# Block attention followed by a token-mixing MLP: another tiling, and an emission order made by a list scheduler

## The chip, the cores and the metric

The kernel runs on one core of one Trainium2 chip. The metric is device time in microseconds. Kernel before: 179.93 us, the median of three runs (179.21 to 181.21).

## The reference, cut to what matters

```python
# q, k, v: (8, 8, 576, 64) fp32; batch 8, heads 8, tokens 576, head size 64
q_c, k_c, v_c = (x.reshape(B, H, 9, 64, 64) for x in (q, k, v))    # chunks of 64 tokens
scores = matmul(q_c, k_c.transpose(0, 1, 2, 4, 3)) / sqrt(64)
attn = exp(scores - max(scores, axis=-1))
attn = attn / (sum(attn, axis=-1) + 1e-09)
x = matmul(attn, v_c).reshape(B, H, S, D).transpose(0, 2, 1, 3).reshape(B, S, 512)

wq, wk = x @ w_q, x @ w_k                                          # w_q, w_k: (512, 64)
W_tok = einsum('bsd,btd->bst', wq, wk) / sqrt(64)
mixed = einsum('bst,btd->bsd', W_tok, x)
out = maximum(mixed, 0.0) @ w_out                                  # w_out: (512, 512), out fp32
```

Both kernels compute the mixing as wq times G, where G = wk^T x is 64 by 512 for each batch, so that no 576 by 576 matrix is made.

## The kernel before

All matmul operands are fp16; inputs are cast by the loads, which POOL issues through its one queue (`load`, lines 77 to 108). A batch's q and k come as runs of two tokens (512 bytes of fp32), its v as runs of one token (256 bytes). Six buffers of q, k and v hold batches 0 to 5; batches 6 and 7 are loaded into buffers that come free. The first two batches are cut into pieces of tiles, each piece with its own transfers for q, k and v and for each half of the heads; weights go between them. The identity for the transposes is made ahead of the first load.

The attention is cut into 36 units. The token rows of four heads (a half, `sl`) are strung together into one row, and a unit is eight 64-token chunks of that row in each of the two halves, 16 blocks of 64 by 64 in all. A unit passes through these stages; two units' first stages are emitted ahead, and the loop over `kk` emits the stages of three neighbouring units in a fixed pattern:

- `stage_a1`, `stage_a2`: 16 transposes of 128 by 64 on TensorE (L327, tile `tp`), one copy of 1,024 columns on VectorE (L337, `qkt`).
- `stage_b1`, `stage_b2`: 16 score matmuls of 64 by 64 (L351, `sp`); maximum (L359, `mx`) and subtraction (L365, `sh`) on VectorE; exponential on ScalarE (L373, `es`).
- `stage_c`: four transposes of 128 by 128 (L380, `ep`) and their copy on ScalarE (L382, `et`).
- `stage_d1`, `stage_d2`: 16 matmuls with v, which has a column of ones that yields the sum (L395, `xp`); sum, reciprocal and product on VectorE (L407, L409, L410, into `x_nat`).

For each batch, the token-mixing part (`make_moe`) follows: transposes of x and copies on ScalarE (L143, L150, `xt`), the projections to wq and wk transposed (L163 and L166, `wpa`, `wpb`; copies L173, L174 into `wqkT`), a copy of wq to the other 64 partitions (L176, `wqd`), ten transposes that turn wk back (L190 to L193, `wknp`; copy L195, `wkn`), G (L205, L209, `gp`; copy L213, `g16`), mixing (L225, `ma`, and L245, `mb`, for the last 64 tokens; relu L131 on ScalarE), and the output projection (L261, `op`; copy L269; tails L281, L289), stored through SyncE's queue from four buffers `osb`. The steps of this part have a period and a place in the loop written out by hand (`plan`, `fill`), with costs in microseconds that decide how many output tiles fit into a period; what is left at the end is emitted by due time.

PSUM: one bank each for `tp`, `sp` and `ep`, two for `xp`, three in rotation for all tiles of the token-mixing part. Every engine runs its instructions in the order of emission.

Of the kernel before, what the change touches and what calls it, by code (L numbers as in the profile page):

```python
# [12 lines left out]
ALU = mybir.AluOpType  # L13
AX = mybir.AxisListType


@with_exitstack
def kernel(
# [10 lines left out]

# [4 lines left out]
    CH = 64  # L38
    P = 128
    HQ = H // 2  # L40
    NC_ = S // CH
    NI = HQ * NC_
    NT = NI // 4
    NS = NI // 2
    NU = B * NI // 8
    R, G = 2, 32
    scale_attn = 1.0 / math.sqrt(D)
    scale_moe = 1.0 / math.sqrt(DH)
    ds = bass.ds

    const = ctx.enter_context(tc.tile_pool(name="const", bufs=1))
    qn_pool = ctx.enter_context(tc.tile_pool(name="qn", bufs=6))
    v_pool = ctx.enter_context(tc.tile_pool(name="vpool", bufs=6))
    qkt_pool = ctx.enter_context(tc.tile_pool(name="qkt", bufs=3))
    sm_pool = ctx.enter_context(tc.tile_pool(name="smp", bufs=3))
    e_pool = ctx.enter_context(tc.tile_pool(name="epool", bufs=3))
    xt_pool = ctx.enter_context(tc.tile_pool(name="xtp", bufs=2))
    moe_pool = ctx.enter_context(tc.tile_pool(name="moep", bufs=2))
    osb_pool = ctx.enter_context(tc.tile_pool(name="osb", bufs=4))

    PS = bass.MemoryType.PSUM
    t_psum = ctx.enter_context(tc.tile_pool(name="tps", bufs=1, space=PS))
    s_psum = ctx.enter_context(tc.tile_pool(name="sps", bufs=1, space=PS))
    et_psum = ctx.enter_context(tc.tile_pool(name="etps", bufs=1, space=PS))
    x_psum = ctx.enter_context(tc.tile_pool(name="xps", bufs=1, space=PS))
    m_psum = ctx.enter_context(tc.tile_pool(name="mps", bufs=3, space=PS))


    ctx.enter_context(tc.manual_schedule())

    ident = const.tile([P, P], F16, name="ident")
    make_identity(nc, ident[:])

    x_nat = const.tile([P, B * NS, 2, D], F16, name="x_nat")
    x_bat = x_nat[:].rearrange("p (b w s) l d -> p b w s l d", b=B, w=2)

    def load(b, cuts):
        qn = [
            qn_pool.tile([P, 2, NT, R * D], F16, name=f"qn{ti}", tag=f"qn{ti}")
            for ti in range(2)  # L80
        ]
        vt = v_pool.tile([P, 2, NS, D + 2], F16, name="vt", tag="vt")
        flat = [
            x[b].rearrange("h s d -> (h s) d").rearrange("(l t p r) d -> l p t (r d)", l=2, p=P, r=R)
            for x in (q, k)
        ]
        vflat = v[b].rearrange("h s d -> (h s) d").rearrange("(l n p) d -> l p n d", l=2, p=P)
        nc.gpsimd.memset(vt[:, :, :, D : D + 1], 1.0)
        if cuts is None:
            for ti in range(2):  # L90
                nc.gpsimd.dma_start(
                    qn[ti][:].rearrange("p l t e -> p (l t) e"),
                    flat[ti].rearrange("l p t e -> p l t e").rearrange("p l t e -> p (l t) e"),
                )
            nc.gpsimd.dma_start(  # L95
                vt[:].rearrange("p l n e -> p (l n) e")[:, :, 0:D],
                vflat.rearrange("l p n d -> p l n d").rearrange("p l n d -> p (l n) d"),
            )
            return qn, vt
        for t0, t1 in cuts:  # L100
            for ti in range(2):
                for sl in range(2):
                    nc.gpsimd.dma_start(qn[ti][:, sl, t0:t1, :], flat[ti][sl, :, t0:t1, :])  # L103
            for sl in range(2):
                nc.gpsimd.dma_start(  # L105
                    vt[:, sl, 2 * t0 : 2 * t1, 0:D], vflat[sl, :, 2 * t0 : 2 * t1, :]
                )
        return qn, vt
# [408 lines left out]
```

## Time and profile before

| what | value |
|---|---|
| time, median of three runs | 179.93 us (179.21 to 181.21) |
| the profiled execution: span from first to last instruction | 177.5 us |
| TensorE matmul busy | 140.1 us (79%), 2,496 instructions |
| VectorE busy | 113.8 us (64%), 239 |
| ScalarE busy | 102.9 us (58%), 203 |
| POOL busy | 55.2 us (31%), 68 |
| transfers of POOL's queue | 76,128 packets, 14.81 MB |
| transfers of SyncE's queue | 5,888 packets, 9.44 MB |

The profiled execution's own time is known by its span alone; the runs' median is 2.4 us more than that span. Busy time of TensorE contains the latency of pipelined matmuls; neighbouring instructions of VectorE and ScalarE overlap by about a tenth of a microsecond, so that distances between starts are shorter than durations. In a line of the timeline stand start, duration, engine, line, operation, tiles, shapes and count, and in brackets the idle time ahead of it with what ended it. In a line of the waits stand who waited for whom, the total in us, how many times, and the longest.

### The profile page before, as it was taken

Reading aid. Unit: us, or ns where it says so; the run is one execution under the profiler, and the core shown is the slowest. Engines: PE = TensorE matmul, PEld = TensorE weight load, DVE = VectorE, ACT = ScalarE, POOL = GpSimd, SP = SyncE. Lnnn points to the kernel's source line nnn. Section 1 sums busy time; section 2 is a strip of 40 time slices with the busy share of each in tenths; the row PEclk is TensorE's granted clock in tenths of the full one; section 3 lists DMA queues with packets and bytes.
Section 4 is the critical chain, followed back from the end, with each engine's and each line's share of the span. In section 5 each row is a group of like instructions: output and inputs, shape, how many; then the busy total and the mean of one; then the engine's idle time right before and its main releaser. Section 6 shows DMA issues by size and latency. Waiting matters only on the chain.

```text
span 177.5 us, 5756 instructions
## 1 busy us (share of the span) xinstructions
PE 140.1 (79%) x2496; PEld 92.2 (52%) x2496; DVE 113.8 (64%) x239; ACT 102.9 (58%) x203; POOL 55.2 (31%) x68
## 2 busy tenths in 40 slices
PE   0364987953977799997997999799979996798990
PEld 0241755842565566665574665566756654454440
DVE  0122869694199778956995988669959865731241
ACT  2001222540548867975797499747956986596630
POOL 8999999916343542422400000000000000000000
PEclk9999999995699999999999999999999999999999
DMA  2999999999999999999999992401303124032435
GB/s 28 98 120 145 112 123 159 185 183 168 177 176 168 182 164 209 231 203 252 178 195 223 173 226 80 151 2 63 94 4 118 60 77 136 0 122 89 177 121 177
DMA packets 82041, 24.62 MB, mean 139 GB/s; under 512 B 76384, under 2 KB 77920, under 8 KB 82016
## 3 DMA queue, kind: packets, MB, share of 16 engines
q0 software_dynamic: 76128, 14.81, 99.1%
q1 hardware_dynamic: 5888, 9.44, 15.5%
q8 instruction: 19, 0.31, 0.7%
q14 instruction: 6, 0.05, 0.1%
HBM read 29.62 MB, written 9.44 MB: 220 GB/s over the span
## 4 chain that ended last, share of the span: by engine, by line
PE 32%; ACT 28%; POOL 17%; DVE 10%; DMA 7%; issue 3%; ACTq 0%; POOLq 0%; DVEq 0%
PE op L261 11%; ACT rmx L131 9%; POOL qn L103 8%; DMA qn<-in_k_dram 7%; ACT xt L150 6%; ACT es L373 5%; POOL vt L105 5%; PE tp L327 4%; PE wpa L163 3%; PE xp L395 2%; ACT et L382 2%; PE ep L380 2%; DVE mx L359 2%; PE sp L351 2%; DVE sh L365 2%
## 5 line engine op out<-in xcount | busy, mean ns | idle before, releaser
L327 PE MATMUL tp<-ident,qn 128*64 128x128 f16 x576 | 30.8, 242 | 17.1 <-DMA qn<-in_q_dram 9.0
L382 ACT COPY et<-ep 128x512 f16<-128x512 f16 x36 | 21.2, 589 | 33.9 <-PE ep L380 33.8
L337 DVE COPY qkt<-tp 128x1024 f16<-128x1024 f16 x36 | 24.6, 682 | 19.1 <-PE tp L327 19.1
L327 PEld LDWEIGHTS <-qn 128*64 128x64 f16 x576 | 21.7, 120 | 25.5 <-DMA qn<-in_q_dram 10.4
L261 PE MATMUL op<-wout,rmx 128*128 128x512 f16 x128 | 31.2, 379 | 0.3 <-ACT xt L148 0.2
L373 ACT ACTIVATE es<-sh 128x512 f16<-128x512 f32 x36 | 22.9, 635 | 13.6 <-DVE sh L365 12.6
L359 DVE TENSOR_REDUCE mx<-sp 128x8 f32<-128x512 f32 x36 | 24.7, 687 | 8.9 <-PE sp L351 8.7
L365 DVE TENSOR_TENSOR sh<-sp,mx 128x512 f32<-128x512 f32 x36 | 24.8, 690 | 2.0
L410 DVE TENSOR_TENSOR x_nat<-xp,rec 128x512 f16<-128x512 f32 x36 | 24.9, 692 | 1.2
L269 ACT COPY osb<-op 128x512 f32<-128x512 f32 x30 | 17.4, 586 | 5.2 <-PE op L261 4.0
L395 PE MATMUL xp<-vt,et 64*64 64x65 f16 x576 | 16.2, 198 | 5.2 <-DVE x_nat L410 3.5
L351 PEld LDWEIGHTS <-qkt 64*64 64x64 f16 x576 | 12.8, 115 | 11.4 <-issue 6.6
L150 ACT COPY xt<-tx 128x768 f16<-128x768 f16 x23 | 18.3, 795 | 0.0
L351 PE MATMUL sp<-qkt 64*64 64x64 f16 x576 | 17.0, 203 | 0.8 <-DVE sh L365 0.8
L131 ACT ACTIVATE rmx<-ma 128x512 f16<-128x512 f32 x30 | 16.5, 610 | 1.2 <-PE ma L225 1.1
L261 PEld LDWEIGHTS <-rmx 128*128 128x128 f16 x128 | 11.6, 98 | 10.4 <-issue 0.2
L395 PEld LDWEIGHTS <-et 64*64 64x64 f16 x576 | 13.0, 113 | 7.3 <-ACT es L373 4.6
L163 PE MATMUL wpa<-xt,wqk 128*128 128x512 f16 x32 | 10.8, 407 | 7.2 <-ACT xt L150 7.2
L95 POOL DMA_DIRECT2D vt<-in_v_dram x6 | 11.0, 1833 | 14.7 <-issue 10.3
L380 PE MATMUL ep<-ident,es 128*128 128x128 f16 x144 | 15.3, 234 | 0.0
L143 PE MATMUL tx<-ident,x_nat 128*128 128x128 f16 x144 | 12.6, 227 | 0.4 <-ACT xt L150 0.3
L176 DVE COPY wqd<-wqkT 64x576 f16<-64x576 f16 x8 | 2.4, 304 | 14.7 <-ACT wqkT L174 14.3
(53 smaller groups left out, 165.8 us busy)
## 6 DMA issues: line engine op xcount, KB each, us to landing
out_dram<-osb SPq DMA_DIRECT2D x32, 256.0 KB, 2.8
qn<-in_q_dram POOLq DMA_DIRECT2D x6, 576.0 KB, 17.1
qn<-in_k_dram POOLq DMA_DIRECT2D x6, 576.0 KB, 18.8
vt<-in_v_dram POOLq DMA_DIRECT2D x6, 576.0 KB, 18.4
out_dram<-osbt SPq DMA_DIRECT2D x16, 64.0 KB, 2.2
wout<-in_moe_w_out_dram POOLq DMA_DIRECT2D x2, 256.0 KB, 8.0
qn<-in_q_dram POOLq DMA_DIRECT2D x4, 96.0 KB, 3.7
qn<-in_k_dram POOLq DMA_DIRECT2D x4, 96.0 KB, 3.5
```

The costliest lines, as they stand in the source:

```text
L131: nc.scalar.activation(to, of, AF.Relu, scale=scale_moe)
L150: nc.scalar.copy(xt[:, 6 * g : 6 * g + 6, :], tx[:])
L261: nc.tensor.matmul(op[:], lhsT=rmx[:, i, ds(t * P, P)], rhs=wout16[:, i, :], start=(i == 0), stop=(i == HQ - 1),)
L327: nc.tensor.transpose(tp[CH * sl : CH * sl + CH, j, ti, :, r, :], src[:, sl, t, r * D : r * D + D], ident[:],)
L337: nc.vector.tensor_copy(qkt[:].rearrange("p j t c k -> p (j t c k)"), tp[:].rearrange("p j t c r g -> p (j t c r g)"),)
L351: nc.tensor.matmul(sp[rows, i, :], lhsT=qkt[rows, j, 0, c, :], rhs=qkt[rows, j, 1, c, :], start=True, stop=True,)
L359: nc.vector.tensor_reduce(mx[:], sp[:], axis=AX.X, op=ALU.max)
L365: nc.vector.tensor_tensor(out=sh[:].rearrange("p i (g r) -> p i r g", g=G, r=R), in0=sp[:].rearrange("p i (r g) -> p i r g", g=G, r=R), in ...
L373: nc.scalar.activation(es[:], sh[:], AF.Exp, scale=scale_attn)
L382: nc.scalar.copy(et[:], ep[:])
L395: nc.tensor.matmul(xv[rows, sl, m, :], lhsT=et[rows, m, CH * sl : CH * sl + CH], rhs=vt[rows, sl, s, 0 : D + 1], start=True, stop=True,)
L410: nc.vector.tensor_tensor(out=x_nat[:, 4 * u : 4 * u + 4, :, :].rearrange("p m l d -> p l m d"), in0=xv[:, :, :, 0:D], in1=rec[:, :, :, No ...
```

## The change

The attention is cut otherwise: a unit is 128 tokens of one batch by all 8 heads (four to a batch, and the last 64 tokens of two neighbouring batches make up one more), again 36 units of 16 blocks. Two units share transposes and copies of q and k. A unit's x then lies as tokens by features, so one group of matmuls gives wq transposed for two units, doubled onto both halves of the partitions by a weight that holds w_q twice, and another gives wk in its natural layout; the copy `wqd` and the transposes of wk are gone. All q, k and v stay in SBUF, v in one tile `v_all` whose ones VectorE writes at the start; the identity is made behind the first four loads. The last 64 tokens of two batches share one output tile. In the last two batches half of the relus and output copies go to VectorE.

No order is written out any more: each step is a `Node` with engine, priority, duration, dependencies, array shape ("form") and PSUM bank, and `plan` builds one order for all engines by simulating them, with assumed landing times for the loads. PSUM is six single banks and one double one, which the planner hands out.

```diff
+def plan(nodes, ring, wides, switch=0.094, sem=0.06, look=0.25):
...
+    def start_of(n):
+        at = max([clock[n.eng]] + [d.done + sem for d in n.deps])
+        slots = []
+        for bk in n.takes:
+            kind = "w" if bk.wide else "r"
+            free = [(t, k) for k, t in free_at.items() if k[0] == kind and k not in held and k not in slots]
+            if not free:
+                return None, None
+            early = [f for f in free if f[0] + sem <= at]
+            t, slot = min(early, key=lambda f: (-f[0], f[1])) if early else min(free)
+            at = max(at, t + sem)
+            slots.append(slot)
+        if n.eng == "PE" and form is not None and form not in n.forms:
+            at = max(at, clock["PE"] + switch)
+        return at, slots
+
+    while left:
+        best = None
+        for e in ready:
+            options = []
...
+            soonest = min(o[0] for o in options)
+            o = min((o for o in options if o[0] <= soonest + look), key=lambda o: (o[1], o[0]))
+            if best is None or o[0] < best[0]:
+                best = o
...
+        clock[n.eng] = at + n.busy
+        n.done = at + n.busy + n.tail
...
+        order.append(n)
...
+    units, tiles = [], {}
+    for b in range(0, B, 2):
+        for bb, ms in ((b, range(NM)), (b, [None]), (b + 1, range(NM))):
+            for m in ms:
+                units.append((bb, m))
...
+    v_all = const.tile([P, NU, H, VW], F16, name="v_all")
+    nc.vector.memset(v_all[:, :, :, D : D + 1], 1.0)
...
+    def pairs(x, b, t0, h0, h1):
+        return x[b, h0:h1, t0 : t0 + 2 * P, :].rearrange("h (p r) d -> p h (r d)", r=R)
...
+    for u in range(NU):
+        b, m = units[u]
+        if m is None:
+            load_rest(u)
+        elif m % 2 == 0:
+            load_pair(u, [(0, 4), (4, 8)] if u == 0 else [(0, 8)])
+        if u == 0:
+            make_identity(nc, ident[:])
+        load_v(u)
+        if u == 2:
+            wq_rows = moe_w_q.rearrange("(f p) j -> p f j", p=P)
+            for i in range(2):
+                nc.gpsimd.dma_start(wq2[:, :, i, :], wq_rows)
+            nc.gpsimd.dma_start(wk1[:], moe_w_k.rearrange("(f p) j -> p f j", p=P))
+        if u == 4:
+            nc.gpsimd.dma_start(wo[:], moe_w_out.rearrange("(f p) n -> p f n", p=P))
...
+    PEd, DVd, ACd = 0.18, 0.09, 0.1
...
+    def turn(form, to, of, i):
+        if form == "full":
+            nc.tensor.transpose(to, of[:, 2 * i : 2 * i + 2, :], ident[:])
+        else:
+            for o in range(2):
+                nc.tensor.transpose(to[CH * o : CH * o + CH], of[:, 2 * i + o, :], ident[:])
...
+    arrive = {}
+    at = 4.5
+    for u in range(NU):
+        b, m = units[u]
+        if m is None:
+            at += 0.75
+        elif m % 2 == 0:
+            at += 2.6
+            arrive["v", u] = at
+        arrive["qk", u] = at
+        at += 0.7
+        arrive["v", u] = at
...
+    LAG = {"tq": -3.0, "S": 0.0, "mx": 0.0, "E": 1.0, "PV": 1.0, "x": 1.0, "xT": 2.0, "pj": 2.0}
...
+            def pe(form, bk=bk, name=name):
+                tp = bank(([P, NF, 4, R, G], F16, "tp"), bk)
+                for j in range(NF):
+                    for r in range(R):
+                        turn(form, tp[:, j, :, r, :], qk[name, u][:, :, r * D : r * D + D], j)
+
+            def ev(bk=bk, name=name, t=t):
+                tt = work.tile([P, NF, 2 * P], F16, name=f"{name}t", tag=f"{name}t", bufs=3)
+                nc.vector.tensor_copy(
...
+        n = add("PE", u + LAG["S"], 16 * 0.017, pe_s, st["qkt_n", u], forms=QUART, takes=[bs], tail=PEd)
+        n = add("DVE", u + LAG["mx"], dve(512), dve_mx, [n], tail=DVd)
+        n = add("DVE", u + LAG["mx"], dve(512), dve_sub, [n], reads=bs, tail=DVd)
+        n = add("ACT", u + LAG["mx"], act(512, True), act_exp, [n], tail=ACd)
+        n = add("PE", u + LAG["E"], 4 * 0.056, pe_e, [n], forms=EITHER, takes=[be], tail=PEd)
+        n = add("ACT", u + LAG["E"], act(512), act_e, [n], reads=be, tail=ACd)
+        n = add("PE", u + LAG["PV"], 16 * 0.017, pe_v, [n, landed(("v", u))], forms=QUART, takes=[bx], tail=PEd)
+        n = add("DVE", u + LAG["x"], dve(512) + 0.36, dve_x, [n], reads=bx, tail=DVd)
...
+            for f in range(NF):
+                nc.tensor.matmul(
+                    pj[:, 0 : n_u * P],
+                    lhsT=wq2[:, f, :, :],
+                    rhs=xt[:, f, :, :],
...
+            for i in range(n_u):
+                for f in range(NF):
+                    nc.tensor.matmul(
+                        pj[:, n_u * P + i * DH : n_u * P + i * DH + DH],
+                        lhsT=xt[:, f, i, :],
+                        rhs=wk1[:, f, :],
...
+        last = b >= B - 2
+        pri = max(mine + [rest]) + (3.0 if b < B - 1 else 2.0)
...
+                    if last and o:
+                        nc.vector.tensor_scalar(to, of, scale_moe, 0.0, op0=ALU.mult, op1=ALU.max)
+                    else:
+                        nc.scalar.activation(to, of, AF.Relu, scale=scale_moe)
...
+                osb = work.tile([P, DM], F32, name="osb", tag="osb", bufs=4)
+                (nc.vector.tensor_copy if vec else nc.scalar.copy)(osb[:], bo.tile[:])
...
+                out_tile(key, evs, a * P, [(0, P, out[b, m * P : m * P + P, :])], pri + 0.5 + 0.8 * m, last and a)
...
+    for n in plan(nodes, 6, 1):
+        n.emit(n.form) if n.eng == "PE" else n.emit()
```

In `plan`, among the steps of an engine whose dependencies are placed, those that could start within `look` of the soonest are candidates, and the one with the lowest priority number is taken; of the engines, the one whose choice starts first places it. A step whose bank is not free is no candidate. The buffers of the SBUF tiles (`qt`, `kt`, `osb` and the rest) are not part of this simulation.

## The prediction

> **What bounds the kernel now.** I read the slices first, then the waits, then the engines by stretch, then TensorE's order of work. The slices of the page (40 equal ones of 4.44 us):
>
> ```profile
> PE   0364987953977799997997999799979996798990
> POOL 8999999916343542422400000000000000000000
> PEclk9999999995699999999999999999999999999999
> DMA  2999999999999999999999992401303124032435
> ```
>
> The loads keep the DMA engines busy to slice 23 (107 us), yet TensorE is short of data only at the start. The waits of the whole span:
>
> ```profile
> PE tp L327 <- DMA qn<-in_q_dram: 9.0, 8, 4.2
> PE wpa L163 <- ACT xt L150: 7.2, 7, 1.5
> PE tp L327 <- DMA qn<-in_k_dram: 7.2, 8, 2.9
> ```
>
> 16.2 us of waits on q and k all lie before 43.3 us; after that the loads are ahead. The stretches that this cuts the span into (first number of each engine: busy us):
>
> ```profile
> 0.00:43.30 43.30, 24.39 (x410) 17.44 (x410) 22.25 (x43) 9.99 (x16) 37.46 (x53) 0.97 1.49 131
> 43.30:60.00 16.70, 14.01 (x285) 10.31 (x286) 11.76 (x26) 10.19 (x21) 6.92 (x6) 0.87 2.07 174
> 60.00:146.00 86.00, 78.55 (x1539) 51.82 (x1535) 68.07 (x144) 64.95 (x132) 10.81 (x9) 1.00 1.10 144
> 146.00:177.50 31.50, 23.12 (x270) 12.59 (x268) 11.71 (x27) 17.73 (x36) 0.00 (x0) 1.00 0.33 116
> ```
>
> In the long third stretch TensorE is at 91%, VectorE at 79%, ScalarE at 76%: TensorE is nearest to being the bound. Its busy time contains latency, though, so I cost each of its groups by the distance from its start to the next one's start, in its timeline:
>
> ```profile
> 98.53 1.89 PE L261 MATMUL op<-wout,rmx 128*128 128x512 f16 x8
> 100.35 0.44 PE L351 MATMUL sp<-qkt 64*64 64x64 f16 x16
> 100.62 0.42 PE L395 MATMUL xp<-vt,et 64*64 64x65 f16 x16
> 101.01 0.64 PE L327 MATMUL tp<-ident,qn 128*64 128x128 f16 x16
> 101.45 0.63 PE L205 MATMUL gp<-x_nat,wkn 128*64 128x256 f16 x8
> 102.02 0.30 PE L209 MATMUL gp<-x_nat,wkn 64*64 64x256 f16 x2
> 102.24 0.40 PE L380 MATMUL ep<-ident,es 128*128 128x128 f16 x4
> 102.48 0.50 PE L143 MATMUL tx<-ident,x_nat 128*128 128x128 f16 x6
> 102.81 1.03 PE L261 MATMUL op<-wout,rmx 128*128 128x512 f16 x4
> ```
>
> So: scores 0.27 us, 16 transposes of q and k 0.44, four of es 0.23, six of x 0.33 (0.056 each). Eight output matmuls took 1.82 and four 0.96 (the next group starts at 103.77), so one is 0.215 and about 0.10 is left over at the change to another array shape (xp 0.39 where its 16 alone are about 0.28). The trace has 168 such changes. The Trainium skill (TensorEngine Tiling (Array Packing), Tiling Modes, Key Properties) says that changing the tiling mode drains the array; by that rule too a price stands on each change, and the trace agrees with its 0.10 us.
>
> All 2,496 matmuls at these prices are 102.6 us, the changes 16.8: 119.4 us of work, and 58 us in which TensorE does not advance. By stretch, work and loss: 12.4 and 30.9; 11.3 and 5.4 (here the granted clock was 0.87); 74.6 and 11.4 (87% used); 21.2 and 10.3.
>
> **TensorE's work after the change.** Two batches are nine units of 128 tokens by 8 heads. Scores 9 x 0.27 = 2.43; values 9 x 0.29 = 2.6; q and k 9 x 0.44 = 3.96; es 9 x 0.23 = 2.07; x 36 x 0.056 = 2.0; outputs 9 x 4 x 0.215 = 7.74, where the 64-token tails of two batches now share one full tile; G 2 x 0.7 = 1.4 (the same ten matmuls); mixing 0.97 (256 columns 0.107 us for two row halves side by side, by L225 pairs that start together at 123.55 and are followed at 123.86). Projections: the ten wknp transposes (0.40 a batch) go; per pair of units come four matmuls of 256 columns (0.43) and eight of 64 columns with 128-column weights. The eight are unseen in a row: a wpb after a long matmul takes 0.03, a wknp 0.04, an x transpose with as wide a weight 0.056; I take 0.04 (the wknp group has the same 64 columns), so 3.38 per nine units, with 1.9 us on either side for all 144. Sum 26.55 per nine units, 106.2 in all: 3.6 more than now. Changes of shape: nine units have 62 groups (9+9+9+9 of attention, 5+5 of projection, 2 G, 5 mixings, 9 outputs); if all differ from the one before, 248 changes; as es and x transposes go in either shape and neighbours agree often, I take 160, 16 us; bounds 126 and 248, -3.4 and +8.8 us. **Work 122.2 us, 2.8 more than now: anything won must come out of the 58 us of loss.**
>
> **The other engines.** VectorE's starts in the timeline near 100 us are 0.60 (max), 0.60 to 0.72 (subtract, longer when it follows its own max), 0.19, 0.24, 0.61 (x) and 0.60 (qkt) apart: some 2.95 us a unit. All stay; L176 and L195 (6.0 us busy) go, and ten 512-column evacuations of the last two batches come (about 6, five more than now). 36 x 2.95 = 106 plus 6. ScalarE: es 0.53, et 0.48, x copies 0.88 a pair (768 columns are 0.68 apart, 512 0.48), projection copies of 384 columns about 0.38 instead of 0.59 and 0.22, outputs and relus 0.48: 24.2 us per nine units against 24.4, 97 in all. Both are below 122, so these edits cost nothing as long as TensorE stays the slowest; VectorE has 0.4 us per unit of cover, and if that is gone the extra shows one for one.
>
> **The loads.** [...]
>
> ```profile
> 40.37 1.81 POOL L95 DMA_DIRECT2D vt<-in_v_dram  x1 [4.37 <-issue]
> 50.56 1.81 POOL L95 DMA_DIRECT2D vt<-in_v_dram  x1 [2.01 <-issue]
> 60.75 1.81 POOL L95 DMA_DIRECT2D vt<-in_v_dram  x1 [2.02 <-PE tx L143]
> ```
>
> 10.2 us a batch. The landings (q 60.44, k 63.71, v 67.45 us) split it: 3.25 for 2,304 runs of 512 bytes, 3.74 for 4,608 of 256. A pair of units (1,024 runs each of q and k, two of v) thus takes 2 x 1.44 + 2 x 0.83 = 4.5 us, a unit of two 64-token tails 3 x 0.83 = 2.5 with its 256-byte runs: 20.6 per two batches against 20.4. The Trainium skill (DMA: Bandwidth & Descriptors, Specifications) wants 512 bytes for line rate; by that the tails' runs are what is lost here, and the trace agrees (0.81 ns against 1.41 ns for half the bytes), but it is under 0.5 us per batch pair.
>
> At the start POOL's issues count (0.74 to 0.9 us each, all three tensors through this one queue). Identity goes behind the first four issues, so the first starts near 0.7 and lands 2.7 later; TensorE can begin near 4.2 and has unit 0 by 6. Then: v of units 0 and 1 at 8, pair 2 at 12.5, weights (three issues, 2.1), the first tail (six issues, 4.4) at 18, wo 2, pairs 5 and 7 at 23.5 and 28, and unit 9's q and k at 32.5, nine units in 30 us where two batches took 35 (last landing 34.84) and TensorE met its last such wait at 43.3. Keeping all inputs frees loads of buffer waits (POOL's waits on PE, 4.4 us, at a time when loads are ahead): worth nothing.
>
> **What the order does to that.** The planner's `arrive` has unit 9's q and k at 24.55. TensorE runs its list in order, so transposes placed there wait 8 us, with everything queued behind them: scores, values and mixing of older units. By then some 12.5 us of work are placed (attention of about six units). From there the placing follows TensorE (over 6 us a pair against 4.5), so loads stay ahead. Stops in that stage also let the clock fall: es transposes took 0.61 us at 31 us and 0.40 at 34. The Trainium skill (TensorE: Matmul & The Clock Gate, Part 1) puts that on idle windows of some 3.4 us and would make all 12.5 us of early work take double; most of that hides in the waits. I add 2 us (0 if the waits hide all, 6 if half of the 12.5 is exposed). **12.5 us of work are done at 34.5.**
>
> **The end.** From the last unit's x, by durations and starts of rows above: transposes 0.4, copy 1.0, projection 0.85, copy 0.5, G 0.9, copy 0.4, mixing 0.4, relu 0.7, five outputs 4.3, copy 0.7, output DMA 2.1, close 0.9: 13.1 us, with 6.5 of TensorE's work in it. The last attention chain before it, from its scores to its x, is about 5 us, of which batch 6's outputs cover some 3: 2 lost.
>
> **Sum.** 34.5 + (122.2 - 12.5 - 6.5) / 0.94 + 2 + 13.1 = 34.5 + 109.8 + 15.1 = 159.4 us of span. The 0.94 is chosen: now 87% in the middle with waits such as wpa on xt in a fixed order per unit; a list built from these very spacings, with six single banks to hand out, should halve that loss, not end it. The median of the runs (179.93) is 2.4 above the profiled span of 177.5; with that, 161.8.
>
> **Rivals.** *The middle stays as lossy* (0.87): 103.2/0.87 = 118.6 and 170.6 us in all. For it: VectorE at 2.95 and TensorE at 3.4 per unit, so each is late for the other; one double bank for the values; osb's four buffers, whose output DMAs land 5.7 us after issue while loads run. Against: 52% use of the six banks by rows (some 10 us of bank time per unit). *The order fits better*: 0.98 and 4 us less of early waiting, 105.3 and 153.3. For it: the planner's constants are the spacings above. *Slower: the order chases the planned loads.* A TensorE slot that nothing older can use is given to the next transposes that `arrive` says have landed; it ends at 74 us where 4.5 us a pair, and 6 beside output writes (76.59 to 86.16 for the last batch), end near 105. If the placing follows `arrive` throughout, TensorE is held at the loads' pace to 105 with 60 us done, and 62/0.94 + 11 + 2.4 more give 184. It decides once TensorE still waits on q or k beyond 75 us. Against: transposes rank three units ahead at most, and qt and kt have three buffers. *It does not do what it says*: v_all is one tile; were each value product to wait for all its loads, nothing could finish before 105 and the time would be over 220. Against: now transposes of the first cut start at 4.18, when later cuts of their tile are not issued.
>
> **Chances.** Forecast 0.42, lossy middle 0.25, better fit 0.21, chasing 0.10, all of v 0.02. The range: from below the better fit (fewer changes of shape, -3) to past the lossy middle with half of a chase, 150 to 176. One per cent is about what a measurement of this kernel can tell; chasing spans both sides of the old time, so faster 0.88, same 0.03, slower 0.09.
>
> **What would show it.** Right: 36 qkt-like copies, 2,600 to 2,800 matmuls with shares as above; TensorE's last wait on q or k between 30 and 42 us; busy 9s from then on; VectorE around 108 us busy; loads ending at 100 to 112. Wrong: waits on q or k past 60 us; a middle with ScalarE or VectorE at 95%; over 200 changes of shape; ScalarE waiting on output DMAs; an end longer than 16 us.

## The result, and the profile after

The kernel after takes 164.98 us (median of four runs, 163.90 to 166.02) where the kernel before took 180.57 beside it: a ratio of 0.916 with a 95% interval of 0.909 to 0.924. The forecast was 161.8 us in a range of 150 to 176. The profiled execution took 165.38 us, its span is 163.6.

The slices of the page (40 of 4.09 us):

```profile
PE   0447559798899989998999999989989997894870
POOL 7999998674998445598672697000000000000000
PEclk9999999999999999999999999999999999999698
DMA  3999999999999999999999999993300422033053
```

Against before's slices the early stretch of 3s, 4s and 6s is shorter: from 25 us on (the seventh digit) TensorE is at 7 to 9 until the end stage begins at 147 us, where before still had a 5 and a 3 in its slices from 35 to 44 us. The loads end at 111 us, 107.6 in before. The granted clock as it is recorded no longer falls at the start; it falls in the last slices instead. TensorE is not quick from its first matmul on all the same: 16 transposes of q or k take 1.07 us at 25.4 us and 0.61 at 30.5, at a recorded clock of 1.00.

TensorE's waits on loads and on what is late at the start, from the list of waits of the whole span (us in total, times, longest):

```profile
PE tp L233 <- POOL ident masks.py:199: 5.0, 1, 5.0
...
PE tp L233 <- DMA qn<-in_q_dram: 4.9, 3, 1.9
...
PE tx L230 <- ACT rm L551: 3.7, 7, 0.7
...
PE tp L230 <- DMA qn<-in_q_dram: 1.9, 1, 1.9
...
PE tp L233 <- DMA kn<-in_k_dram: 0.8, 2, 0.5
```

Waits on q and k are 7.6 us where they were 16.2, and the last of them ends at 25.4 us where it was 43.3. The stretches that answer to the prediction's (duration, then busy us of TensorE, its weight loads, VectorE, ScalarE, GpSimd; granted clock):

```profile
0.00:34.50 34.50, 19.15 (x408) 16.04 (x409) 16.99 (x33) 8.65 (x13) 30.85 (x43) 1.00 1.68 142
34.50:60.00 25.50, 23.27 (x451) 16.39 (x449) 21.33 (x44) 20.31 (x36) 17.77 (x22) 1.00 1.89 184
60.00:148.50 88.50, 82.47 (x1666) 58.94 (x1665) 69.30 (x145) 70.56 (x132) 28.82 (x36) 1.00 1.14 152
148.50:163.60 15.10, 8.44 (x58) 3.96 (x57) 3.70 (x6) 3.58 (x7) 0.00 (x0) 0.85 0.31 106
```

By the prediction's own prices (start-to-start of each kind of matmul, 0.10 us for each change of shape) the trace holds 105.0 us of matmuls and 144 changes, 119.4 us of work; the same count for before is 102.2 and 168, 119.0. **The work is the same to about a microsecond. The gain is loss that went: 58.5 us before, 44.2 after.** Divided at 60 us: 36.4 before and 26.4 after in the first stretch, 22.1 and 17.8 behind it. So 13.9 us of span are 10.0 from the start, 4.3 from the rest, less 0.4 of work. This division is used for every kernel below; a profile is one execution, so a us of it either way means little.

Two things shift it. The prediction's 0.04 us for a product of 64 columns is too much; eight of them take 0.23 us, 0.029 each, as two lines of the timeline of after show:

```profile
143.34 0.40 PE L457 MATMUL pj<-wk,xt 128*128 128x64 f16 x8
143.57 1.03 PE L567 MATMUL op<-wo,rm 128*128 128x512 f16 x4
```

At that price the work of after is 117.8 us and its losses are some 26.8 and 19.0, so that the part behind 60 us gains some 3 and not 4.3; the other kernels with these 144 products shift as after does, and only before, before_batch1_whole and wk_by_transposes are without them. And the last 20 output matmuls took 6.1 to 6.4 us in the profiled executions of after, true_landings and wk_by_transposes and 5.3 in that of vector_pad; in the others of the table that end with 20 of them they took 4.48. third_batch_k_last runs the same list as after and has 4.48. Up to 1.9 us of the loss behind 60 us is therefore of the execution and not of the kernel.

| kernel | median, us | ratio to before (95%) | span | work | loss to 60 us | loss behind 60 us | k of the third batch's first unit lands |
|---|---|---|---|---|---|---|---|
| before | 180.57 | 1 | 177.5 | 119.0 | 36.4 | 22.1 | 43.2 (whole batch) |
| before_batch1_whole | 177.49 | 0.992 (0.989–0.994) | 175.7 | 119.0 | 35.9 | 20.8 | 41.3 (whole batch) |
| after | 164.98 | 0.916 (0.909–0.924) | 163.6 | 119.4 | 26.4 | 17.8 | 35.0 |
| third_batch_k_last | 171.38 | 0.953 (0.943–0.964) | 168.2 | 119.4 | 31.3 | 17.5 | 40.6 |
| small_first_loads | 180.99 | 1.010 (1.006–1.014) | 179.1 | 119.4 | 40.5 | 19.1 | 51.2 |
| wk_by_transposes | 171.41 | 0.951 (0.941–0.961) | 169.3 | 118.2 | 27.9 | 23.2 | 34.8 |
| vector_pad | 168.53 | 0.942 (0.936–0.947) | 166.4 | 120.8 | 27.7 | 17.9 | 35.4 |
| longer_chain | 177.60 | 0.985 (0.977–0.994) | 175.8 | 119.9 | 29.4 | 26.4 | 36.1 |
| priority_order | 201.84 | 1.125 (1.119–1.132) | 199.6 | 122.2 | 32.9 | 44.5 | 35.9 |
| true_landings | 160.39 | 0.890 (0.882–0.898) | 159.0 | 119.8 | 22.1 | 17.1 | 36.1 |
| wout_later | 160.45 | 0.888 (0.885–0.892) | 159.3 | 120.7 | 22.5 | 16.0 | 32.8 |
| wout_later_split_end | 159.17 | 0.887 (0.882–0.891) | 157.0 | 120.7 | 21.2 | 15.1 | 33.4 |

Each ratio is against the kernel before on the same chip; it leaves out executions in the chip's slower state (over 1.5% above the fastest of the same kernel), which the medians keep. The landings are read as they stand in the trace (us from the start of the span).

### The profile page after: what moved, and what is told of

The parts are those of the page before. It is cut to its first block, busy times and chain, and to the rows that moved or that the text cites. A ratio compares the mean times of both kernels' runs of the same rounds, so it can differ in the third digit from the quotient of the medians.

```text
span 163.6 us, 5896 instructions
## 1 busy us (share of the span) xinstructions
PE 133.3 (81%) x2576; PEld 95.3 (58%) x2576; DVE 111.3 (68%) x227; ACT 103.1 (63%) x187; POOL 77.4 (47%) x100
## 4 chain that ended last, share of the span: by engine, by line
PE 39%; DVE 24%; ACT 15%; POOL 10%; DMA 4%; issue 4%; DVEq 0%; ACTq 0%; POOLq 0%
PE op L567 16%; DVE sh L360 8%; DVE mx L346 6%; DVE xs L408 5%; ACT rm L551 5%; PE xp L393 4%; DMA kn<-in_k_dram 4%; ACT es L370 4%; PE tp L233 3%; PE tx L230 3%; ACT xt L441 3%; PE sp L336 3%; PE pj L448 3%; POOL v_all L195 2%; POOL qn L176 2%
## 5 line engine op out<-in xcount | busy, mean ns | idle before, releaser
L567 PE MATMUL op<-wo,rm 128*128 128x512 f16 x144 | 37.8, 392 | 0.5 <-DVE rm L549 0.5
L370 ACT ACTIVATE es<-sh 128x512 f16<-128x512 f32 x36 | 23.2, 644 | 18.3 <-DVE sh L360 13.1
L195 POOL DMA_DIRECT2D v_all<-in_v_dram x32 | 28.6, 912 | 1.9 <-DMA v_all<-in_v_dram 1.8
L408 DVE TENSOR_TENSOR xs<-xp,rec 128x512 f16<-128x512 f32 x36 | 24.9, 691 | 1.2
L360 DVE TENSOR_TENSOR sh<-sp,mx 128x512 f32<-128x512 f32 x32 | 22.1, 689 | 2.6 <-ACT xt L441 0.5
L551 ACT ACTIVATE rm<-ma 128x512 f16<-128x512 f32 (+1 forms) x35 | 20.3, 683 | 1.4 <-PE ma L531 1.4
L567 PEld LDWEIGHTS <-rm 128*128 128x128 f16 x144 | 13.2, 100 | 13.1 <-issue 2.2
L441 ACT COPY xt<-tx 128x1024 f16<-128x1024 f16 (+1 forms) x20 | 18.7, 934 | 2.7 <-PE tx L230 2.1
L233 PE MATMUL tp<-ident,qn 128*64 128x128 f16 x256 | 11.7, 239 | 9.9 <-POOL ident masks.py:199 5.0
L393 PE MATMUL xp<-v_all,et 64*64 64x65 f16 x576 | 16.8, 198 | 2.2 <-ACT et L381 0.7
L176 POOL DMA_DIRECT2D kn<-in_k_dram x17 | 15.1, 886 | 5.5 <-DMA kn<-in_k_dram 4.5
L176 POOL DMA_DIRECT2D qn<-in_q_dram x17 | 15.3, 901 | 2.6 <-DMA qn<-in_q_dram 1.1
```

What stands on the lines that cost most here:

```text
L176: nc.gpsimd.dma_start(qk[name, u][:, h0:h1, :], pairs(x, b, m * P, h0, h1))
L195: nc.gpsimd.dma_start(v_all[:, u, :, 0:D], rows(v, b, m * P, P))
L233: nc.tensor.transpose(to[CH * o : CH * o + CH], of[:, 2 * i + o, :], ident[:])
L360: nc.vector.tensor_tensor(out=sh[:].rearrange("p i (g r) -> p i r g", r=R), in0=sp[:].rearrange("p i (r g) -> p i r g", r=R), in1=mx[:, :, ...
L370: nc.scalar.activation(es[:], st["sh", u][:], AF.Exp, scale=scale_attn)
L393: nc.tensor.matmul(xv[r, h // 4, h % 4, :], lhsT=et[r, j, CH * hp : CH * hp + CH], rhs=v_all[r, u, h, 0 : D + 1], start=True, stop=True,)
```

## The experiments

### The start: in which order the same bytes come

In the kernel before, q of the third batch landed at 40.0 us, k at 43.24: one transfer each for four and a half units. In the kernel after, q and k of the third batch's last unit land at 43.6 us, as late, but unit 9, its first, has both at 35.0. Three runs change the landings alone.

**third_batch_k_last** issues the third batch's loads as before did, with nothing else changed:

```
(in words)
-    unit by unit: q and k of the pair or tail, then v
+    units 9 to 13: q of 9, 11, 13; then k of 13, 11, 9; then all v
```

> The kernel after, with the same list, and with the q and k of units 9 to 13 (the third batch) loaded as batches were before: all of q, then all of k with unit 9's last, then all of v; the same bytes in the same stretch of the queue. From the landings of the profile after (32.1 us for unit 8's v, then 1.43 us for each q or k of a pair, 0.8 to 0.9 for one of the tail) unit 9's k lands near 38.8 instead of 35.0, unit 13's v still near 44.4. Theory (before 60 us TensorE runs its list in order, so the first transfer of a batch counts by its landing, and transfers by unit instead of by batch are where the start was won): 3 to 4 us slower than after, 168 to 169, all of it as waits on q or k between 32 and 40 us. Rival (as when w_out was moved: what is lost at one place of the start is made up by 60 us, only the bytes up to some later unit count): at most 1 us slower, 164.5 to 166.

Measured: unit 9's k landed at 40.6 us (38.8 expected), unit 13's v at 45.0 (44.4), and the ratio went from 0.916 to 0.953, 6 us or so; the profiled spans differ by 4.6, with 4.9 more in the loss to 60 us, and with the last outputs 1.6 us shorter as said above. The theory is right in kind; the cost is larger than the 3 to 4 us expected, as the landing is later too (5.6 us). In after TensorE did not stop for unit 9's k: its transposes start at 35.88 us, 0.87 behind the landing. Here they start at 40.68, 4.8 us later, which is the loss. Its waits, one line of TensorE's timeline, TensorE and its clock in the slices, and two stretches:

```profile
PE tp L249 <- DMA qn<-in_q_dram: 5.7, 3, 2.5
...
PE tp L249 <- DMA kn<-in_k_dram: 4.3, 3, 3.5
```

```profile
40.68 1.06 PE L249 MATMUL tp<-ident,kn 128*64 128x128 f16 x16 [3.50 <-DMA kn<-in_k_dram]
```

```profile
PE   0536738683889998998899899998998999796670
...
PEclk9999999965699999999999999999999999999999
```

```profile
34.50:38.00 3.50, 2.68 (x60) 2.14 (x54) 3.33 (x8) 1.91 (x3) 2.85 (x4) 0.57 2.05 171
38.00:42.00 4.00, 1.32 (x18) 1.09 (x19) 1.36 (x3) 0.00 (x0) 3.51 (x6) 0.50 2.29 160
```

TensorE stands 3.5 us in front of unit 9's k with everything older queued behind it, and around that stop the granted clock shows 5 and 6, as it did in the profile before at the same place. The Trainium skill (TensorE: Matmul & The Clock Gate, Part 1) puts the clock at half after an idle window of some 3.4 us; the trace agrees with the stop of 3.50 us and 0.50 in that stretch, though the clock was already at 0.57 from 34.5 to 38 us, ahead of it.

**small_first_loads** cuts the loads of the first nine units smaller:

```
-            load_pair(u, [(0, 4), (4, 8)] if u == 0 else [(0, 8)])
+            load_pair(u, [(h, h + 2) for h in range(0, 8, 2)] if u < 9 else [(0, 8)])
```

and v of these units in two halves.

> The changed kernel with the loads of the first nine units cut into more transfers, as the kernel before had them (q and k of a pair of units in eight, v of a unit in two): POOL then needs some 42 us to issue what took it 24, and unit 9's k lands at 45 to 47 us instead of 35. Start theory (10 us of the change's gain are the earlier loads): the delay counts nearly one for one, 172 to 177 us. Rival, older units' token mixing fills the time: 166 to 169.

Measured: unit 9's k landed at 51.2 us, 16.2 later and not the 10 to 12 expected, and the time rose by 16.0 us, above the 172 to 177 expected; that is the whole gain. Its waits:

```profile
PE tp L235 <- DMA qn<-in_q_dram: 11.9, 13, 1.8
...
PE tp L232 <- DMA qn<-in_q_dram: 4.6, 1, 4.6
```

Behind 60 us it loses 19.1 us, 1.3 more than after. **before_batch1_whole** loads the second batch of the kernel *before* in whole transfers instead of two cuts (`load(1, None)`):

> The kernel before with batch 1 loaded in three transfers instead of twelve: POOL has batch 2 issued some 6 us earlier. Start theory: TensorE's last wait for k moves from 43 us to 36 to 39 and the time by about as much: 174 to 176.5 us against 180. Rival, the fixed order of periods takes the time back or the first piece of batch 1 now comes later: 178.5 to 181.

Measured: the third batch's k landed 2.0 us earlier, not the 4 or more expected, and the span is 1.8 us shorter (time ratio 0.992). The size was missed: POOL issued the third batch's q 5.8 us earlier (23.32 us where it was 29.14), yet it landed 1.6 us earlier. The rate was about one for one.

So in these three runs the time follows the landing of the third batch's first unit, about one for one, in both kernels. Of the 10.0 us won before 60 us, undoing the order of the third batch alone gives back 4.9; the first nine units, all landed at 32.1 us where two batches were at 34.84, are a further 2.7 by their landings alone, which no run takes apart; 2.4 are not assigned.

### The list: what it believes of the landings, and whether its clock matters

**true_landings** replaces the planner's `arrive` by the landings that the trace of after shows:

```
-    arrive = {}
-    at = 4.5
...
+    qk_lands = {0: 7.7, 2: 13.5, 4: 18.5, 5: 25.4, 7: 30.0, 9: 35.0, ...}
+    v_lands = [9.0, 10.1, 14.3, 16.5, 19.4, 26.3, 27.1, 31.6, 32.1, ...]
+    arrive = {("qk", u): t ...} | {("v", u): t ...}
```

> The changed kernel with the planner's table of landings replaced by the landings that its own trace shows (unit 9's k at 35.0 us instead of 24.6, the last at 109.5 instead of 74). Order theory: part of the 10 us in which TensorE stands at q and k up to 30 us is filled with older work: 162 to 164 us against 165.0. Rival, the landings themselves bind the start and there is no older work to place: 164.5 to 165.5. If the order had been chasing the planned loads further on, 160 or less.

Measured: 160.39 us, 4.6 faster, more than the 1 to 3 expected, 4.3 of it in the loss to 60 us, although unit 9's k landed 1.1 us *later* than in after. Of TensorE's waits on loads one is left:

```profile
PE tp L233 <- DMA qn<-in_q_dram: 1.4, 1, 1.4
```

By 34.5 us it had done 15.6 us of work against 11.7: older work stands in front of the waits and not behind them. The wrong arrivals thus cost 4 to 5 us, more than the 2 that the prediction had for them.

**priority_order** keeps the same steps and priorities and drops the simulated clock: the ready step with the lowest priority is placed next.

```
-            soonest = min(o[0] for o in options)
-            o = min((o for o in options if o[0] <= soonest + look), key=lambda o: (o[1], o[0]))
-            if best is None or o[0] < best[0]:
+            o = min(options, key=lambda o: (o[1], o[0]))
+            if best is None or (o[1], o[0]) < (best[1], best[0]):
```

> The changed kernel with a planner that takes, of all steps whose inputs and bank are placed, the one of the lowest priority number, whatever its clock says: the same software pipeline without a simulated time. Scheduler theory: the clock is what packs the middle, TensorE's use there falls to the 0.86 of the kernel before or less, 170 to 178 us. Layout theory: the priorities alone give the same overlap and the gain comes from loads and banks: 164 to 168.

Measured: 201.84 us, 12.5% slower than before and far over the 170 to 178 expected. Three of its waits:

```profile
PEld L566 <- ACT rm L550: 12.3, 8, 3.4
...
PE op L566 <- ACT rm L550: 12.0, 6, 3.7
...
PE pj L447 <- ACT xt L440: 11.9, 18, 1.3
```

Each step of a chain is placed straight behind the one that it needs, so TensorE waits for ScalarE again and again (18 times for xt, with 20 projections). The clocked list is worth 37 us against this. What it is worth against the order that was written by hand no run measures.

### The projections: what lies behind 60 us

**wk_by_transposes** gives the units back the old way to q- and k-weights: one product of 128 columns, a copy to the other half of the rows, a transpose of k's half and its copy; everything else stays.

```
-    (eight matmuls pj[... DH] <- xt, wk1; wq2 holds q's weights twice)
+    wd = work.tile(...); nc.vector.tensor_copy(wd[CH:P, :], wt[0:CH, :])
+    nc.tensor.transpose(wp[:, i, :], wt[CH:P, i * P : i * P + P], ident[CH:P, CH:P])
+    nc.vector.tensor_copy(wk[:], wp[:])
```

> The changed kernel with its projections undone: one weight that holds w_q and w_k side by side, wq copied to the other 64 partitions on VectorE, wk turned by transposes (two a pair) and copied on VectorE; all of it planned as nodes. Loss theory (the gain of the change is time in which TensorE stood still, 10 us of it at the start and 4 in the middle): eight matmuls of 64 columns go and two transposes and changes of shape come, VectorE has the room, the chain at the end gets about 1 us longer: 164 to 167.5 us. Rival, the removed copies and transposes are what brings the gain: 170 or more.

Measured: 171.41 us, 6.4 slower, so the rival (170 or more) is right. By the table 5.4 of it is in the loss behind 60 us, some 4.5 with the 64-column products at 0.029 us; that loss is with 23.2 back at before's 22.1. TensorE's work is 1.2 us less by the prediction's prices (products 4.3 less, 31 more changes of shape 3.1 more), and about the same at 0.029 us. The two large groups of copies (busy us, mean ns; then idle before them):

```profile
L461 DVE COPY wqd<-wt 64x256 f16<-64x256 f16 x16 | 4.2, 260 | 3.5 <-ACT wt L455 3.0
...
L475 DVE COPY wkn<-wknp 128x128 f16<-128x128 f16 x16 | 3.5, 222 | 1.3 <-PE wknp L471 0.9
```

So the new projections, which the prediction had as a cost in matmuls and otherwise as nothing, are worth at least as much as the stretch behind 60 us gained. It is not the same loss that comes back, though. Before's 7.2 us of TensorE's waits for x transposed (wpa on xt) stay away; in after and then in wk_by_transposes the wait of the projections on xt is:

```profile
PE pj L448 <- ACT xt L441: 1.2, 1, 1.2
```

```profile
PE pj L445 <- ACT xt L438: 1.3, 2, 1.1
```

By what way does the edit cost? **vector_pad** adds 40 copies of that size to VectorE that nobody reads (two per projection, from the evacuated tile).

```
+        add("DVE", pri, dve(128 * n_u, 2), pad(CH, 128 * n_u, "pad_a"), [n], tail=DVd)
+        add("DVE", pri, dve(64 * n_u, 2), pad(P, 64 * n_u, "pad_b"), [n], tail=DVd)
```

> The changed kernel with 40 more VectorE copies (of 64 by 256 or 128 by 128, two for each projection, planned as nodes) whose results nobody reads: the VectorE time of the run that brought the copies of wq and wk back, 9.4 us busy there, without their place in the chain and without TensorE's transposes. That run took 171.4 us against 165.0. VectorE theory: VectorE has no room of its own, so its time alone costs 4 to 7 us: 169 to 172. Chain theory: the longer way from the projection to G and the mixing is what cost, and copies beside it cost nothing: 164 to 166.5.

Measured: 3.5 us slower by the medians and some 4.5 by the ratios (0.942 against 0.916), so at the lower edge of the VectorE theory or just under it. In the profile 2.9: 1.4 is 14 more changes of shape in the list, 1.3 lies before 60 us, and the loss behind 60 us hardly moves (17.9; some 0.9 us up if the shorter last outputs are counted). Time on VectorE alone then does not fill that stretch; a list that comes out different with every edit is part of what these runs measure. **longer_chain** does the other half: three copies of a single column, VectorE, ScalarE, VectorE, one behind the other between a projection's evacuation and its use.

```
+        for eng, took, copy, tail in (
+            ("DVE", dve(1), nc.vector.tensor_copy, DVd),
+            ("ACT", act(1, True), nc.scalar.copy, ACd),
+            ("DVE", dve(1), nc.vector.tensor_copy, DVd),
+        ):
+            n = add(eng, pri, took, again(copy), [n], tail=tail)
```

> The kernel after with three single-column copies, one behind the other, VectorE, ScalarE, VectorE, between a projection's evacuation and its use by G and the mixing (20 projections, 60 copies; each rewrites one column of the evacuated tile with itself; the planner is told of them). They take under 0.2 us of an engine each, so some 6 us of VectorE and 4 of ScalarE over the span, and no TensorE, but make the chain from projection to G about 1 us longer, as the transposes and copies do that wk_by_transposes brings back (0.3, 0.26 and 0.22 us of busy time and three hand-overs; that cost 6.4 us, of which the trace puts 5.4 of loss behind 60 us). Theory (the length of the chain from x to the outputs costs, not the time of VectorE): 3 us or more slower than after, 168 to 170. Rival (the chain is hidden in the middle, where the list has older and younger work to place, and shows at the end alone, once): 0.7 to 1.5 us slower, 165.7 to 166.5, and what wk_by_transposes lost in the middle was the time of its copies and its worse fit.

Measured: 177.60 us, 12.6 slower, twice what the transposes and copies cost, and far over both expectations. 8.6 us of it are loss behind 60 us, nearly all before 140. VectorE's waits show what stands in its order of work; of before:

```profile
DVE qkt L337 <- PE tp L327: 19.1, 6, 7.2
DVE wqd L176 <- ACT wqkT L174: 14.3, 7, 3.6
```

of longer_chain, and then one of these waits in its timeline:

```profile
DVE den L405 <- PE xp L393: 18.1, 17, 2.4
...
DVE qt L314 <- PE tp L233: 11.6, 4, 5.3
...
DVE wt L481 <- ACT wt L467: 9.6, 9, 2.6
```

```profile
112.46 0.62 PE L230 MATMUL tx<-ident,xs 128*128 128x128 f16 x8
...
114.73 1.06 ACT L441 COPY xt<-tx 128x1024 f16<-128x1024 f16 x1
...
116.70 0.48 ACT L467 CAST wt<-pj 128x384 f16<-128x384 f32 x1
...
117.21 0.16 DVE L481 COPY wt<-wt 128x1 f16<-128x1 f16 x1 [2.59 <-ACT wt L467]
...
118.61 0.69 DVE L346 TENSOR_REDUCE mx<-sp 128x8 f32<-128x512 f32 x1 [0.63 <-PE sp L336]
```

VectorE stood 2.59 us in front of a copy of 0.16 us. The lateness lies at the head of the chain: the transposes of x ended at 113.08, and ScalarE came to their copy at 114.73, behind relus and an output copy; the products then ended at 116.67, and their evacuation began at once. The next maximum was not held by the small copies: it waited 0.63 us more, for its scores. In before it was the copy L176 that stood so, 14.3 us in seven batches; in vector_pad it is 10.3 us, in wk_by_transposes 3.0; in after VectorE has no instruction that waits for a projection's evacuation at all. That this stand is there in each kernel that has such a step is shown. That it is what costs is not: 9.5 of vector_pad's 10.3 us lie behind 60 us, where it loses hardly more than after, and the costs (6.4, 3.5, 12.6 us) do not go by these waits.

Three more things were in longer_chain. The planner had the small copies at 0.07 and 0.09 us and they took 0.151 and 0.207, so it placed what followed too early. TensorE has 7.4 us of stops for which the profile names no releaser (0.6 in after). And TensorE was slower: the granted clock was 0.91 from 80 to 100 us and 0.83 from 100 to 120, where after had 1.00. Eight output matmuls of longer_chain and then of after:

```profile
108.49 3.59 PE L580 MATMUL op<-wo,rm 128*128 128x512 f16 x8
```

```profile
144.90 1.90 PE L567 MATMUL op<-wo,rm 128*128 128x512 f16 x8
```

Of the 8.0 us that longer_chain loses more than after between 60 and 140 us, some 4.7 are matmuls that stand further apart without a stop ahead of them. So the 12.6 us are not the price of a longer chain alone, and how much belongs to each stays open.

### What was not the reason

**relu_rows** lets the relu of the mixing read PSUM across columns and write its rows straight, where after writes with a stride:

```
-                        to = to.rearrange("p (c g r) -> p c r g", g=G, r=R)
-                        of = of.rearrange("p (c r g) -> p c r g", g=G, r=R)
+                        to = to.rearrange("p (c g r) -> p c g r", g=G, r=R)
+                        of = of.rearrange("p (c r g) -> p c g r", g=G, r=R)
```

> The changed kernel with its 512-column relus walking the tokens in another order: they read PSUM in strides and write SBUF without gaps, as the kernel before did. Bank theory: in the changed kernel two such relus start 0.58 us apart where the kernel before had 0.49 and the planner assumes 0.48; TensorE waits 3.7 us for the mixing banks that they empty. With 0.49 the waits fall to 1 or 2 us, span 2 to 4 us shorter: 161 to 163 us against 165.0. Rival, the relus lie beside other work and the bank is only the last of several things to come free: 164.5 to 165.5.

Measured: ratio 0.915 (0.907 to 0.922) against 0.916, no change, though ScalarE is 2.5 us less busy. In the trace TensorE's waits on rm fall from 3.7 to 2.3 us, and the time does not follow.

**k_copy_on_scalar**, on true_landings, gives every second pair's copy of k to ScalarE (`nc.scalar.copy` in place of `nc.vector.tensor_copy`).

> The changed kernel with the true landings in its planner (160.4 us) and the copy of k's transposes moved to ScalarE for every second pair of units: VectorE's starts sum to 0.15 us a unit less (2.80), ScalarE's to 0.22 more (2.91). VectorE theory: VectorE was nearest to TensorE's pace, 1 to 3 us come off: 157.5 to 159.5. Rival, the two engines wait for TensorE and the chain alike: 160 to 162.

Measured: 161.91 us, ratio 0.902 (0.897 to 0.908) against 0.890: no gain, rather a loss. VectorE fell from 111.8 to 107.8 us busy and ScalarE rose from 103.5 to 110.9, so VectorE's busy time is not the bound.

### Two steps further

**wout_later** moves w_out's load, on true_landings, from behind unit 4's v to behind unit 10's, and sets the landings to suit.

```
-        if u == 4:
+        if u == 10:
             nc.gpsimd.dma_start(wo[:], moe_w_out.rearrange("(f p) n -> p f n", p=P))
```

> true_landings with the load of w_out issued behind unit 10's v instead of behind unit 4's, and the planner's landings of units 5 to 9 set to what that gives (about 3 us earlier). Theory (the start counts one for one: span minus the landing of unit 9's k is set by the kernel, 122.9 us in true_landings): unit 9's k lands near 32.5 to 33 instead of 36.1, the time falls by about 3 us, to 157 to 158. Rival (the first ten units' loads are no longer what TensorE waits for once the landings are right, or the first output products, at 36.3 us in true_landings, now wait for w_out): 160 to 161.5, with a wait of op on w_out in the list.

Measured: unit 9's k landed at 32.8 as expected, and the time is 160.45: the rival is right. By 34.5 us it had 2.0 us more work done than true_landings, at 60 us 0.4 less. Unit 11's k lands at 39.9 (40.7), and w_out now at 37.0; the first output products start at 37.08, behind a stop of 1.32 us that the profile puts down to ScalarE's rm. The same step in the kernel next below shows a wait for w_out:

```profile
37.66 1.04 PE L558 MATMUL op<-wo,rm 128*128 128x512 f16 x4 [1.34 <-DMA wo<-in_moe_w_out_dram]
```

The one-for-one rule thus does not hold for a transfer that is made to come sooner at the cost of the next. The planner knows nothing of w_out's landing; a list that is told of it was not tried.

**wout_later_split_end** projects the last two units one by one; their mixing then takes wq from two tiles, which have one buffer more:

```
+        elif u == NU - 1:
+            project([u - 1])
+            project([u])
```

> wout_later with the last two units projected one by one instead of as a pair, so that the last x passes through half as wide a copy (384 instead of 768 columns before the projection, 192 instead of 384 after it). Theory (the end is a chain of single steps, each waiting for the one before: tx, copy, pj, copy, G): some 0.5 us off the two copies, less 0.2 for more shape changes and small groups; 0.3 to 1 us faster than wout_later, and the wait of pj on xt at the end shorter than the 1.16 us in the profile after. Rival (what ends last is the output products and relus behind it, or the extra instructions take it back): within 0.3 us of wout_later.

Measured: 159.17 us, the fastest of all; its interval overlaps that of wout_later, so the times do not tell them apart. The chain at the end is shorter. The last unit's transposes and products, of after and then of this kernel:

```profile
146.64 0.61 PE L230 MATMUL tx<-ident,xs 128*128 128x128 f16 x8
148.41 0.60 PE L448 MATMUL pj<-xt,wq 128*128 128x256 f16 x4 [1.16 <-ACT xt L441]
...
149.80 0.30 PE L493 MATMUL gp<-xs,wt 64*64 64x256 f16 x2 [0.57 <-ACT wt L467]
...
152.36 6.12 PE L567 MATMUL op<-wo,rm 128*128 128x512 f16 x20 [0.51 <-DVE rm L549]
```

```profile
142.90 0.39 PE L230 MATMUL tx<-ident,xs 128*128 128x128 f16 x4
144.02 0.38 PE L439 MATMUL pj<-xt,wq 128*128 128x128 f16 x4 [0.73 <-ACT xt L432]
...
144.93 0.30 PE L484 MATMUL gp<-xs,wt 64*64 64x256 f16 x2 [0.41 <-ACT wt L458]
...
147.48 4.48 PE L558 MATMUL op<-wo,rm 128*128 128x512 f16 x20 [0.50 <-DVE rm L540]
```

From the last unit's x (142.06 us here, 146.36 in after) to the outputs it is 5.4 us; in after, true_landings and wout_later it is 6.0. That lies within the 0.3 to 1 us expected. This is the fastest of the kernels tried: ratio 0.887 to before.

## Why the prediction was right, and where it was not

**The start was right in most of its steps.** 12.5 us of work at 34.5 us were forecast, 11.7 were done; the last wait on q or k was to lie between 30 and 42 us and ended at 25.4, outside that sign of being right. Unit 9's k was put at 32.5 and landed at 35.0: the pace of 4.5 us a pair nearly held (4.6 and 5.0), the issues at the start and w_out (landed 22.5) were slower. The planned arrivals did make the transposes wait; the chasing rival (184 us) needed such waits beyond 75 us and is refuted.

**TensorE's work** was to be 122.2 us, 2.8 more than now; it is 119.4. The matmuls were put at 106.2 and are 105.0 by the same prices, most of the difference being G: put at 0.7 us a batch, its ten matmuls take 0.47 and 0.12 once the two changes of shape among them are counted apart. With the 64-column products at 0.029 us instead of 0.04 they are 103.4. The changes of shape were put at 160 and are 144. VectorE was to be about 108 us busy and is 111.3. The 2,576 matmuls are just below the 2,600 to 2,800 named.

**The middle came out by two errors that cancel.** It was to use TensorE at 0.94 and used it at 0.89 (101.2 us of work from 34.5 to 148.5), nearer to the lossy rival's 0.87; with the 64-column products at 0.029 us it is 0.88. But there was less work, and 34.5 + 109.8 + 2, the time at which the last unit's x was to be there, is 146.3; it was there at 146.36. That agreement is luck.

**The step that failed is "these edits cost nothing as long as TensorE stays the slowest; VectorE has 0.4 us per unit of cover".** The copies L176 and L195 were counted by their busy time, 6.0 us, and set to nothing because VectorE has room. Bringing back the old way to wq and wk, copies and transposes together, costs 6.4 us, so room on VectorE was no reason for nothing. Copies of that size on VectorE alone cost 3.5 to 4.5 us, hardly any of it in the loss behind 60 us. What the rest is, the longer chain, the transposes with their changes of shape, or a list that comes out worse, stays open. VectorE's own list of waits in the profile before has 14.3 us in front of L176, six times its busy time of 2.4 us, and was not read; but vector_pad has waits of the same kind and does not lose by them, so that row is not shown to be the price either.

**The end was 4 us too short:** 13.1 forecast, 17.2 measured from the last x to the close. The chain to the outputs took 6.0 us against 5.2. The five output tiles took 6.2 us instead of 4.3, beside a granted clock of 0.79 to 0.81 (4.5 us in third_batch_k_last, whose list is the same, and in wout_later and wout_later_split_end, where it stayed up); the last copy and its DMA took 3.6 instead of 2.8, the close 1.4 instead of 0.9. Against that the time outside the span was 1.8 us, not 2.4: the 2.4 took the span of one execution from the median of several, and every execution on record, of before too, has 1.7 to 1.8. An end from 16 us on was named as a sign of a wrong prediction. After's end is past it; with the same list third_batch_k_last has 15.6.

**Which rival was near.** The better fit (153.3) counted on the planner's constants; its wrong landings alone cost 4.6 us of that. With landings that are right, and a list planned anew from them, the middle still loses 7 us from 60 to 140.

## What to carry to other kernels

Do not set a step to nothing because its engine has room: copies and transposes whose removal was given no price cost 6.4 us when they were put back, on a VectorE that was 68% busy. Busy time and waits of that engine each suggest a price; a run that puts the step back measures it. Where loads set the start, the order in which the same bytes land counted about one for one in three runs, so issue what the first step of the next stage needs ahead of the rest; a list that is planned at build time should be fed with landings from a trace (4.6 us here). Before a planner's order is credited with a gain, take away one part of the change at a time. And look at the granted clock before a difference in loss is put down to the order of work.

## What the runs showed of the hardware that was not expected

The granted clock fell in the end stage of after (0.79 from 150 to 154 us, 0.81 to 158.6) though TensorE's longest stop there was 1.16 us; in third_batch_k_last, with the same list, it stayed at 1.00 over the last outputs. Within a stretch in which everything that it needs is there, TensorE at times stops with no releaser that the profile shows, as in wout_later:

```profile
48.31 0.25 PE L327 MATMUL sp<-kt,qt 64*64 64x64 f16 x4 [0.98 <-issue]
```

It comes to 0.6 us in after, 7.4 in longer_chain, in places that differ from kernel to kernel; no run here tells why. On ScalarE, four relus of 512 columns that read PSUM straight and write with a stride took 2.49 us; read with a stride and written straight, in relu_rows, they took 2.04.
